# Router logits by token quarters, turned by VectorE, in a fused retention and mixture-of-experts kernel

## The chip, the cores and the metric

The kernel runs on one core of a Trainium2 chip. The metric is the device time of one execution in microseconds (us), lower is better; times are medians of several runs on the same chip. The engines are TensorE (PE, matmuls; PEld is its loading of weights), VectorE (DVE), ScalarE (ACT), GpSimd (POOL) and SyncE (SP, which here issues DMAs).

## The reference

Eight batches and eight heads of retention (attention with a decay in place of the softmax), then a mixture of experts over the 4608 tokens, in which each expert takes at most 576:

```python
ret = scores * Dmat                       # scores = q k^T / 8, Dmat = gamma_h ** (i - j) for i >= j
x = (ret @ v) in the order (batch, token, head * dim)      # 4608 x 512
logits = x @ w_gate                       # 4608 x 8
for idx in np.argsort(-logits.flatten()): # greedy, best pair of token and expert first
    tok, e = idx // E, idx % E
    if assigned[tok] >= 0 or counts[e] >= cap: continue
    assigned[tok] = e; counts[e] += 1
for e in range(E):
    mask = assigned == e
    out[mask] = np.maximum(x[mask] @ w1[e], 0.0) @ w2[e]
```

## The kernel before

**Attention** works on four batch pairs (bp) of two batches, each with four head pairs (hp) of two heads: 16 units u = 4 bp + hp, each in two half units, h = 2u + g, numbered 0 to 31. One half unit makes on TensorE the outputs from the running states (`from_states`), the scores of the next blocks (`scores`), two steps of the state (`update`) and the outputs from masked scores (`from_blocks`). VectorE multiplies the scores with the decay (`masks`, tile `am`, in even halves also `at`), ScalarE copies states (`st`) and outputs (`keep`, into the transposed outputs `xT`), GpSimd scales queries (`qin`) and keys (`ks`) two units ahead. The states of an odd half are multiplied into the same bank from which `at` has to be read first. The loads of a unit are issued by SyncE four units ahead, in one order with the writes of finished rows.

**What else is to be done in a half unit** stands in the table `fill`: `at(h, f, ...)` puts a call behind the work of half h (h - 0.5: ahead of its copy). For each finished batch pair bp these calls, from half g = 8 (bp + 1) on, turn the outputs into rows (`rows`, VectorE, two blocks of 128 tokens into one of four `raw` buffers), write these to the scratch array xd (`rows_out`, SyncE), and make the **logits** of its nine token blocks: `logits` multiplies three blocks at a time, each head pair into its own 32 partitions of a PSUM bank, and copies that with ScalarE into `lt`; `logits2` transposes it with TensorE, and VectorE sums the four head pairs into `Lg` [token in block, block, expert]. Then `best` (six VectorE steps: highest logit, its expert), `count_tables` (tables G of how many candidates each token reaches), `count_first_pe` (nine matmuls that count them), `first_digits` and `first_table` (digits of the logits and tables FT for the search). The last batch pair goes through the same steps behind the last half unit, with nothing beside them.

**Routing and experts.** `search_first` finds the threshold of the first expert by digits, `members` and `listing` number its tokens (a token's number is 128 times its block plus its partition), rows are gathered from xd, and `moe` does the eight expert layers, with the search for the next expert on VectorE beside the matmuls. Their order is written by a small planner with fixed costs.

Of the kernel before, what the change touches and what calls it, by code (L numbers as in the profile page):

```python
# [66 lines left out]
def route_consts():  # L67
    p = np.arange(128)

    def ordered(k, sh):  # L70
# [4 lines left out]
    rows = lambda a: np.broadcast_to(a.reshape(1, -1), (128, a.size))  # L75
    f = np.concatenate([p[:, None] < p[None, :], p[:, None] > p[None, :], rows(8 - np.arange(8)), rows(np.arange(32)),
                        rows(32*(4*(np.arange(20) % 5) + np.arange(20)//5)), rows(np.arange(36)),
                        rows(np.append(ordered(128, FIRST[0])[1:], np.finfo(np.float32).max)), rows(np.arange(1, 129)),
                        p[:, None]], axis=1)
# [6 lines left out]
class Route:  # L86
# [14 lines left out]
    def setup(s):  # L101
# [32 lines left out]
        s.pc = take(1)  # L134
        s.Gt = T("G0", [9, 128], BF16)
# [292 lines left out]
    def listing(s, p):  # L428
# [16 lines left out]
        for g0, g1 in ((0, 9),) if p else ((0, 5), (5, 9)):  # L445
# [3 lines left out]
            if p:  # L449
                V.tensor_scalar(rh[:, 1, :, c], rh[:, 2, :, c], s.pc, None, op0=ALU.mult)  # L450
            else:
                nc.scalar.activation(rh[:, 1, :, c], rh[:, 2, :, c], AF.Copy, scale=s.pc)
# [17 lines left out]
        for a in range(4):  # L470
            V.scalar_tensor_tensor(s.idx[32*a:32*a+32], lo[:, 0, 0, 5*a:5*a+5], 128.0, lo[:, 0, 1, 5*a:5*a+5], op0=ALU.mult, op1=ALU.add)
        if early:
            s.room(cn)
        if p >= PIECES:
            s.quarter = pool.tile([128, 20], I32, name="quarter", bufs=2)
            V.tensor_scalar(lo[:, 1], lo[:, 0], 4.0, None, op0=ALU.mult)
            for a in range(4):
                V.scalar_tensor_tensor(s.quarter[32*a:32*a+32], lo[:, 1, 0], 128.0, lo[:, 1, 1], op0=ALU.mult, op1=ALU.add)
                if a:
                    V.tensor_scalar(s.quarter[32*a:32*a+32], s.quarter[32*a:32*a+32], float(a), None, op0=ALU.add)  # L480
# [48 lines left out]
def attention(tc, nc, P, qk, vk, cst_d, wg_d, rf, xd, Lg, raw):  # L529
# [45 lines left out]
    R = Route(P['c'], P['a'], P['ps'], Lg, P['ident'])  # L575
# [96 lines left out]
    def logits(bp, b0, b1):  # L672
        lt = LT[bp, b0] = P['w'].tile([128, 640], F32, name="lt", bufs=1)
        for z0, z1 in ((b0, b1),) if b1 - b0 < 5 else ((b0, 6.5), (6.5, b1)):
            z0, z1 = int(128*z0), int(128*z1)
            pl = bank("pT", [128, z1 - z0])
            for i, (x, y, b) in enumerate(runs(z0, z1)):
                for hp in range(HP):
                    nc.tensor.matmul(pl[32*hp:32*hp+32, x-z0:y-z0], wg[:, hp, b, :], XT[bp][:, hp, x:y],  # L679
                                     start=(i == 0), stop=True, skip_group_check=True)  # L680
            nc.scalar.activation(lt[:, z0-128*b0:z1-128*b0], pl, AF.Copy)

    def logits2(bp, b0, b1):
        lt = LT[bp, b0]
        n, c0 = b1 - b0, bp*NB + b0
        pt = bank("pT", [128, n, 4, 32]) if n < 5 else here[0].rearrange("p x q -> p (x q)")[:, :128*n].rearrange("p (j h e) -> p j h e", h=4, e=32)
# [555 lines left out]
```

## Time and profile before

| | |
|---|---|
| median of 3 runs | 630.12 us (628.62 to 633.43) |
| profiled execution | 635.54 us, span 633.8 us, 14777 instructions |
| mean granted TensorE clock | 0.983 |
| TensorE busy | 603.6 us, 95% of the span |
| VectorE, ScalarE, GpSimd busy | 428.5, 257.2, 240.5 us |
| DMA in the first 160 us | 48.31 MB, 302 GB/s on the mean |

The profile is of one execution, which took longer than the three timed ones. Busy shares are means over stages with different limits: the first 145 us are attention, the rest is routing and experts. Full speed of TensorE's clock is 1.00; it has two levels, 1.2 and 2.4 GHz.

### The profile page before, as it was taken

Reading aid. Unit: us, or ns where it says so; the run is one execution under the profiler, and the core shown is the slowest. Engines: PE = TensorE matmul, PEld = TensorE weight load, DVE = VectorE, ACT = ScalarE, POOL = GpSimd, SP = SyncE. Lnnn points to the kernel's source line nnn. Section 1 sums busy time; section 2 is a strip of 40 time slices with the busy share of each in tenths; the row PEclk is TensorE's granted clock in tenths of the full one; section 3 lists DMA queues with packets and bytes.
Section 4 is the critical chain, followed back from the end, with each engine's and each line's share of the span. In section 5 each row is a group of like instructions: output and inputs, shape, how many; then the busy total and the mean of one; then the engine's idle time right before and its main releaser. Section 6 shows DMA issues by size and latency. Waiting matters only on the chain.

```text
span 633.8 us, 14777 instructions
## 1 busy us (share of the span) xinstructions
PE 603.6 (95%) x5724; PEld 518.4 (82%) x5724; DVE 428.5 (68%) x1506; ACT 257.2 (41%) x449; POOL 240.5 (38%) x295
## 2 busy tenths in 40 slices
PE   7899998998999999999999999999999895999995
PEld 5788887775698889879978987997898694989984
DVE  6746868888889888878867875885787641453400
ACT  2344432342553545535452562555162331343310
POOL 5787555405411541532431342143127566021011
PEclk9999998999999999999999999999999997899998
DMA  9999899845877698696993898499477423240011
GB/s 327 407 377 397 280 353 322 264 121 168 205 205 160 208 265 201 212 269 146 240 229 113 189 234 233 87 244 238 141 154 214 154 87 95 72 166 25 1 36 40
DMA packets 51225, 124.83 MB, mean 197 GB/s; under 512 B 7187, under 2 KB 22419, under 8 KB 51155
## 3 DMA queue, kind: packets, MB, share of 16 engines
q1 hardware_dynamic: 37906, 80.10, 36.7%
q0 software_dynamic: 13104, 43.53, 30.5%
q8 instruction: 45, 0.74, 0.5%
q10 hardware_dynamic: 144, 0.26, 0.1%
q14 instruction: 26, 0.20, 0.1%
HBM read 80.35 MB, written 18.87 MB: 157 GB/s over the span
## 4 chain that ended last, share of the span: by engine, by line
PE 54%; issue 17%; DMA 15%; POOL 8%; DVE 3%; SPq 1%; ACT 0%; POOLq 0%; DVEq 0%
PE ph L1061 23%; PE py L1102 21%; DMA vin<-in_vk 8%; POOL xg L981 6%; DMA xd<-raw 2%; POOL out_y L1079 2%; DMA kin<-in_qk 2%; DMA qin<-in_qk 2%; PE r L353 2%; PE pt L1025 2%; PE sc L603 1%; PE px L647 1%; DMA raw<-in_w 1%; PE pT L679 1%; PE pS L624 1%
## 5 line engine op out<-in xcount | busy, mean ns | idle before, releaser
L1102 PE MATMUL py<-w2h,hb 128*128 128x512 f32 x576 | 187.8, 398 | 1.1 <-issue 1.1
L1061 PE MATMUL ph<-xh,w1h 128*128 128x320 f32 (+1 forms) x512 | 153.2, 303 | 2.0 <-issue 1.7
L1061 PE MATMUL ph<-xl,w1h 128*128 128x320 f32 (+1 forms) x512 | 150.8, 299 | 3.1 <-issue 3.1
L1061 PE MATMUL ph<-xh,w1l 128*128 128x320 f32 (+1 forms) x512 | 150.4, 299 | 2.8 <-issue 2.7
L1102 PE MATMUL py<-w2l,hb 128*128 128x512 f32 (+1 forms) x320 | 125.1, 391 | 0.9 <-issue 0.9
L1102 PEld LDWEIGHTS py<-w2h,hb 128*128 128x128 f32 x576 | 104.4, 188 | 24.6 <-issue 3.2
L1061 PEld LDWEIGHTS ph<-xl,w1h 128*128 128x128 f32 x512 | 97.3, 192 | 5.3 <-issue 5.1
L1061 PEld LDWEIGHTS ph<-xh,w1h 128*128 128x128 f32 x512 | 97.3, 192 | 4.6 <-issue 3.3
L1065 ACT ACTIVATE hb<-ph 128x256 fp32r<-128x256 f32 (+1 forms) x128 | 51.6, 409 | 117.5 <-PE ph L1061 99.9
L1061 PEld LDWEIGHTS ph<-xh,w1l 128*128 128x128 f32 x512 | 97.2, 192 | 1.6 <-issue 1.6
L1079 POOL DMA_INDIRECT out_y<-yt,idx x40 | 40.5, 1011 | 148.2 <-ACT yt L1119 90.6
L1068 DVE SCALAR_TENSOR_TENSOR hb<-ph,hb 128x256 fp32r<-128x256 f32 (+1 forms) x192 | 57.7, 351 | 43.0 <-ACT hb L1065 39.5
L1102 PEld LDWEIGHTS py<-w2l,hb 128*128 128x128 f32 (+1 forms) x320 | 56.7, 177 | 13.4 <-issue 0.7
L588 POOL TENSOR_TENSOR qin<-qin,cst 128x512 f32<-128x512 f32 (+1 forms) x48 | 47.1, 1009 | 42.3 <-DMA qin<-in_qk 38.3
L1119 ACT ACTIVATE yt<-py 128x512 f32<-128x512 f32 x32 | 19.1, 598 | 99.1 <-PE py L1102 60.4
L612 DVE TENSOR_TENSOR am<-sc,cst 128x1024 f32<-128x1024 f32 x32 | 39.1, 1221 | 29.3 <-PE sc L603 29.1
L627 ACT ACTIVATE st<-pS,cst 128x128 f32<-128x128 f32 x64 | 23.5, 368 | 80.0 <-PE pS L624 80.0
L962 POOL DMA_DIRECT2D w2l<-raw x24 | 21.7, 905 | 71.9 <-ACT w2l L961 32.1
L993 POOL DMA_INDIRECT xg<-xd,idx x30 | 30.2, 1005 | 43.0 <-DVE room L494 16.1
L981 POOL DMA_INDIRECT xg<-xd,quarter x36 | 36.5, 1013 | 12.9 <-issue 10.7
L603 PE MATMUL sc<-qin,kin 64*128 64x128 f32 x512 | 38.1, 289 | 1.7 <-POOL qin L588 1.4
L962 POOL DMA_DIRECT2D w1l<-raw x23 | 21.2, 935 | 43.5 <-ACT w1l L961 35.1
(196 smaller groups left out, 943.4 us busy)
## 6 DMA issues: line engine op xcount, KB each, us to landing
raw<-in_w SPq DMA_DIRECT2D x56, 512.0 KB
w2l<-raw POOLq DMA_DIRECT2D x24, 512.0 KB
w1l<-raw POOLq DMA_DIRECT2D x23, 512.0 KB
qin<-in_qk SPq DMA_DIRECT2D x14, 576.0 KB
kin<-in_qk SPq DMA_DIRECT2D x14, 576.0 KB
vin<-in_vk SPq DMA_DIRECT2D x14, 576.0 KB
nin<-in_vk SPq DMA_DIRECT2D x14, 512.0 KB
xd<-raw SPq DMA_DIRECT2D x36, 128.0 KB
```

Of the source, the lines that this page charges most:

```text
L588: nc.gpsimd.tensor_tensor(x, x, e[:, None, :n].to_broadcast([128, (b-a)//n, n]), op=ALU.mult)
L603: nc.tensor.matmul(t[:, h, 128*j:128*j+128], blk(k, 4*g+j)[r], blk(q, 4*g+j)[r], start=(j == 0), stop=True, skip_group_check=True)
L612: nc.vector.tensor_tensor(a, SC[u, g].rearrange("p h (j q) -> p h j q", q=128), m1[:, u % HP, :, None, :].to_broadcast([128, 2, 4, 128]), ...
L627: nc.scalar.activation(s, p, AF.Copy, scale=ss[:, u % HP, c:c+1])
L962: add = lambda: nc.gpsimd.dma_start(lo, raw, accum_op=ALU.add)
L981: nc.gpsimd.indirect_dma_start(out=t[:, k, :], out_offset=None, in_=xq[:, :], in_offset=bass.IndirectOffsetOnAxis(ap=quarters[e][:, v:v+1] ...
L993: nc.gpsimd.indirect_dma_start(out=xg[:n, j, :], out_offset=None, in_=xd[:, :], in_offset=bass.IndirectOffsetOnAxis(ap=found[e][:n, j:j+1] ...
L1061: T.matmul(ps, w, x, start=(k == 0), stop=(k == 11))
L1065: A.activation(hb[:, f, c], ps, AF.Relu)
L1068: V.scalar_tensor_tensor(hb[:, f, to+a:to+b], ps[:, a:b], 0.0, hb[:, f, 256*s+a:256*s+b].bitcast(F32), op0=ALU.max, op1=ALU.subtract)
L1079: st = nc.gpsimd.indirect_dma_start(out=out[:, :], out_offset=bass.IndirectOffsetOnAxis(ap=found[e][:n, t:t+1], axis=0), in_=y[:n], in_off ...
L1102: T.matmul(ps[:m], a, w, start=(k == 0), stop=(k == last), skip_group_check=True)
```

## The change

The logits of a batch pair are made by token quarters. In a first step (z = 0) the pair's first 512 tokens go as four groups of 128 columns into four groups of 32 partitions, in a second (z = 1) the other 640 as four groups of 160; the four head pairs are added in PSUM. One turn of 32x32 squares by VectorE (`turned`) brings the result into `Lg`, whose rows are now 32 wide, with 8 in use. The copy by ScalarE, the transposes by TensorE and the sums are gone. Tokens lie in another order over partitions and columns, so the numbers for the lists change (`blocks()`, `p % 32`, 32 in place of 128). The tables G share the buffer of the later ones.

In the table `fill`, `best` comes into half g + 5 (it was at the front of g + 6), the tables G into g + 6, 6, 7, the digits into g + 7 (it was g + 8), the tables FT up to one half earlier. For the third pair all of that stands two halves earlier still, in one piece for nine blocks, and its turns into rows begin one half earlier. The logits of the last pair's first three head pairs are put into halves 27, 28 and 30; only those of the fourth remain behind its outputs.

```diff
-    def logits(bp, b0, b1):
-        lt = LT[bp, b0] = P['w'].tile([128, 640], F32, name="lt", bufs=1)
-        for z0, z1 in ((b0, b1),) if b1 - b0 < 5 else ((b0, 6.5), (6.5, b1)):
-            z0, z1 = int(128*z0), int(128*z1)
-            pl = bank("pT", [128, z1 - z0])
-            for i, (x, y, b) in enumerate(runs(z0, z1)):
-                for hp in range(HP):
-                    nc.tensor.matmul(pl[32*hp:32*hp+32, x-z0:y-z0], wg[:, hp, b, :], XT[bp][:, hp, x:y],
-                                     start=(i == 0), stop=True, skip_group_check=True)
-            nc.scalar.activation(lt[:, z0-128*b0:z1-128*b0], pl, AF.Copy)
-
-    def logits2(bp, b0, b1):
...
-        for j in range(n):
-            nc.tensor.transpose(pt[:, j], lt[:, j*128:(j+1)*128], ident)
-        nc.vector.tensor_reduce(Lg[:, c0:c0+n, :], pt[:, :, :, 0:8].rearrange("p j h e -> p j e h"), axis=AX.X, op=ALU.add)
+    def logits(bp, z, hps=range(HP)):
+
+        if z == 0 and 0 in hps:
+            LT[bp] = P['ps'].tile([128, 288], F32, name="lt", tag="t", bufs=1)
+        x, n, o = ((0, 128, 0), (512, 160, 128))[z]
+        for hp in hps:
+            for g in range(4):
+                nc.tensor.matmul(LT[bp][32*g:32*g+32, o:o+n], wg[:, hp, g // 2, :], XT[bp][:, hp, x+n*g:x+n*g+n],
+                                 start=(z == hp == 0), stop=True, skip_group_check=True)
+
+    def turned(bp, z0, z1):
+        a, b = (0, 4)[z0], (4, 9)[z1]
+        nc.vector.transpose(Lg[:, bp*NB+a:bp*NB+b].rearrange("p c e -> p (c e)"), LT[bp][:, 32*a:32*b])
...
-        n = 6 if end else 9
-        digits, best = R.first_digits(c, c+n), R.best(c, c+n)
+        digits, best = R.first_digits(c, c+9), R.best(c, c+9)
...
-        for h, x in ((1, (0, 1)), (2, (2, 3)), (3, (4, 5)), (4, (6, 7)), (5, (8,))):
+        for h, x in enumerate(((0, 1), (2, 3), (4, 5), (6, 7), (8,)), not end):
...
+        for z in range(2):
+            at(g+z, logits, bp, z)
+        at(g+2, turned, bp, 0, 1)
         for i in range(3):
-            at(g+2*i, logits, bp, 3*i, 3*i+3)
-            at(g+2*i+1, logits2, bp, 3*i, 3*i+3)
-            at(g + ((4, 5, 6) if end else (6, 7, 7))[i], R.count_tables, c+3*i, c+3*i+3)
+            at(g + ((4, 4, 5) if end else (6, 6, 7))[i], R.count_tables, c+3*i, c+3*i+3)
         for i in range(6):
-            fill[g + (4 if end else 6)].insert(i, (next, (best, None)))
-        if end:
-            last = R.best(c+6, c+9)
-            for i in range(6):
-                fill[g+6].insert(i, (next, (last, None)))
...
+            at(g + (3 if end else 5), next, best, None)
...
+    for hp in range(HP - 1):
+        for z in range(2):
+            at(27 + hp + (hp == 2), logits, NP-1, z, (hp,))
...
-    logits2(bp, 0, 4)
-    logits(bp, 4, 9)
+    logits(bp, 1, (HP-1,))
+    turned(bp, 0, 0)
     rest(R.count_first(27, 31))
+    turned(bp, 1, 1)
     R.first_table(3, 4, 6)
     here[0] = P['pp'].tile([128, 2, 512], F32, name="px", tag="px", bufs=2)
-    logits2(bp, 4, 9)
```

VectorE in halves 21 and 22, the second batch pair, before (`raw` is the turn of block 8, `Lg` the sum of logits, `am` and `at` the masks, m to oh the six steps of `best`, G a counting table):

```order
L700 STREAM_TRANSPOSE raw<-xT 128x4x4x32
L689 TENSOR_REDUCE Lg<-pT 128x24
L612 TENSOR_TENSOR am<-sc,cst 128x1024
L616 TENSOR_TENSOR at<-px,cst 128x256
L211 TENSOR_REDUCE m<-Lg 128x9
L213 TENSOR_TENSOR t_468<-Lg,m 128x72
L215 TENSOR_TENSOR t_468<-t_468,decb 128x72
L219 TENSOR_SCALAR m<-m 128x9
L221 TENSOR_REDUCE mx_469<-t_468 128x9
L223 TENSOR_TENSOR oh<-t_468,mx_469 128x72
L238 TENSOR_TENSOR G_493<-rc_f,m 128x384
L612 TENSOR_TENSOR am<-sc,cst 128x1024
```

The same place in the changed kernel:

```order
L700 STREAM_TRANSPOSE raw<-xT 128x4x4x32
L216 TENSOR_REDUCE m<-Lg 128x9
L218 TENSOR_TENSOR t_468<-Lg,m 128x72
L220 TENSOR_TENSOR t_468<-t_468,decb 128x72
L224 TENSOR_SCALAR m<-m 128x9
L226 TENSOR_REDUCE mx_469<-t_468 128x9
L228 TENSOR_TENSOR oh<-t_468,mx_469 128x72
L617 TENSOR_TENSOR am<-sc,cst 128x1024
L621 TENSOR_TENSOR at<-px,cst 128x256
L243 TENSOR_TENSOR G<-rc_f,m 128x384 x2
L617 TENSOR_TENSOR am<-sc,cst 128x1024
```

The six steps of `best` moved from behind the masks of half 22 to ahead of them; the sum of logits is gone.

TensorE in the last half unit and behind it, before (px from `am` and `at` are the last outputs, G the counts of the third pair, xT at the end the row transposes of the last pair):

```order
L679 MATMUL pT<-xT,wg 32x256 x8
L647 MATMUL px<-am,vin 64x128 x8
L653 MATMUL px<-at,vin 64x64 x4
...
L688 MATMUL pT<-ident,lt 128x128 x4
L679 MATMUL pT<-xT,wg 32x320 x8
L688 MATMUL px<-ident,lt 128x128 x5
L718 MATMUL pT<-ident,xT 128x128 x16
```

And in the changed kernel, from the logits of the third head pair in half 30 on:

```order
L684 MATMUL lt<-xT,wg 32x128 x4
L684 MATMUL lt<-xT,wg 32x160 x4
L643 MATMUL px<-qin,st 64x128 x8
L643 MATMUL px<-qin,st 64x64 x4
L684 MATMUL lt<-xT,wg 32x128 x4
L652 MATMUL px<-am,vin 64x128 x8
L658 MATMUL px<-at,vin 64x64 x4
L684 MATMUL lt<-xT,wg 32x160 x4
L718 MATMUL pT<-ident,xT 128x128 x16
```

Nine transposes and three of four parts of the last pair's logits left the place behind the last outputs; the counts of the third pair moved ahead of the last half.

## Rows read from the trace of the kernel before

**Rows 1.** Busy us and counts by stretch; then granted clock, DMA share, GB/s.

```profile
90.00:100.00 10.00, 7.24 (x147) 6.38 (x150) 4.84 (x9) 3.10 (x8) 6.24 (x6) 0.98 1.02 352
100.00:110.00 10.00, 9.94 (x189) 8.69 (x189) 9.76 (x18) 3.04 (x7) 5.22 (x7) 0.85 1.00 310
```

**Rows 2.** Timeline of PE, second pair: start us, us, instructions, [idle before].

```profile
81.15 0.86 PE L679 MATMUL pT<-xT,wg 128*32 128x128 f32 x16
81.94 0.78 PE L638 MATMUL px<-qin,st 64*64 64x128 f32 x24
...
85.47 0.55 PE L688 MATMUL pT<-ident,lt 128*128 128x128 f32 x3
85.94 0.45 PE L638 MATMUL px<-qin,st 64*64 64x128 f32 x8
...
89.13 0.86 PE L679 MATMUL pT<-xT,wg 128*32 128x64 f32 x16
...
109.32 0.78 PE L638 MATMUL px<-qin,st 64*64 64x128 f32 x24
...
114.23 0.45 PE L638 MATMUL px<-qin,st 64*64 64x128 f32 x8
```

**Rows 3.** Chain that ended last, up to the hole: start us, us, what.

```profile
80.66 8.66 DMA vin<-in_vk
...
89.34 8.10 DMA xd<-raw
```

**Rows 4.** Timeline of all engines around the hole.

```profile
93.92 0.45 PE L638 MATMUL px<-qin,st 64*64 64x128 f32 x8
...
97.56 0.71 DVE L700 STREAM_TRANSPOSE raw<-xT 128x512 f32<-128x512 f32 x1 [3.96 <-DMA xd<-raw]
98.19 0.22 DVE L689 TENSOR_REDUCE Lg<-pT 128x24 f32<-128x96 f32 x1
...
98.33 1.21 DVE L612 TENSOR_TENSOR am<-sc,cst 128x1024 f32<-128x1024 f32 x1
98.88 2.93 POOL L588 TENSOR_TENSOR qin<-qin,cst 128x512 f32<-128x512 f32 x3 [2.96 <-DMA qin<-in_qk]
...
99.80 0.20 DVE L211 TENSOR_REDUCE m<-Lg 128x9 f32<-128x72 f32 x1
...
99.93 1.34 PE L638 MATMUL px<-qin,st 64*64 64x128 f32 x24 [2.76 <-DVE at L616]
...
100.30 1.15 DVE L215 TENSOR_TENSOR t<-t,decb 128x72 bf16<-128x72 bf16 x1
...
101.77 2.04 POOL L593 TENSOR_TENSOR ks<-nin,cst 128x512 f32<-128x512 f32 x2
102.00 0.90 DVE L223 TENSOR_TENSOR oh<-t,mx 128x72 bf16<-128x72 bf16 x1
...
104.91 0.45 PE L638 MATMUL px<-qin,st 64*64 64x128 f32 x8
```

**Rows 5.** Timeline of DVE, first and last of the six steps, third pair.

```profile
125.27 0.19 DVE L211 TENSOR_REDUCE m<-Lg 128x6 f32<-128x48 f32 x1
...
126.19 0.21 DVE L223 TENSOR_TENSOR oh<-t,mx 128x48 bf16<-128x48 bf16 x1
```

**Rows 6.** Timeline from the last half unit to the search.

```profile
133.38 0.93 PE L638 MATMUL px<-qin,st 64*64 64x128 f32 x24
134.23 1.26 PE L679 MATMUL pT<-xT,wg 128*32 128x256 f32 x16
...
136.81 0.77 ACT L662 ACTIVATE xT<-px 128x320 f32<-128x320 f32 x2 [0.67 <-DVE FT L198]
...
139.74 1.04 PE L718 MATMUL pT<-ident,xT 128*128 128x128 f32 x8
...
142.01 0.37 PE L247 MATMUL px<-oh,G 128*128 128x8 bf16 x9
...
142.42 0.17 DVE L252 TENSOR_TENSOR f<-px,room 128x8 bf16<-128x8 f32 x1
```

More of the change, by code (lines that the diff above doesn't have):

```diff
@@ L75, in route_consts, with blocks @@
     rows = lambda a: np.broadcast_to(a.reshape(1, -1), (128, a.size))
+    def blocks():
+        c, g = np.arange(36)[None, :], p[:, None] // 32
+        z = c % 9
+        return 36*(c // 9) + np.where(z < 4, 4*g + z, 16 + 5*g + z - 4)
     f = np.concatenate([p[:, None] < p[None, :], p[:, None] > p[None, :], rows(8 - np.arange(8)), rows(np.arange(32)),
-                        rows(32*(4*(np.arange(20) % 5) + np.arange(20)//5)), rows(np.arange(36)),
+                        rows(32*(4*(np.arange(20) % 5) + np.arange(20)//5)), blocks(),
                         rows(np.append(ordered(128, FIRST[0])[1:], np.finfo(np.float32).max)), rows(np.arange(1, 129)),
-                        p[:, None]], axis=1)
+                        p[:, None], p[:, None] % 32], axis=1)
     return np.ascontiguousarray(f, dtype=np.float32)
@@ L133, in setup @@
         s.dec, i32, i20, cc, s.cand128, k128 = [take(n) for n in (8, 32, 20, 36, 128, 128)]
-        s.pc = take(1)
-        s.Gt = T("G0", [9, 128], BF16)
+        s.pc, s.pm = take(1), take(1)
+        s.Gt = s.G.rearrange("p (a b) k -> p a (b k)", a=9)
         V.tensor_copy(s.decb, s.dec)
@@ L449, in listing @@
             if p:
-                V.tensor_scalar(rh[:, 1, :, c], rh[:, 2, :, c], s.pc, None, op0=ALU.mult)
+                V.tensor_scalar(rh[:, 1, :, c], rh[:, 2, :, c], s.pm, None, op0=ALU.mult)
             else:
-                nc.scalar.activation(rh[:, 1, :, c], rh[:, 2, :, c], AF.Copy, scale=s.pc)
+                nc.scalar.activation(rh[:, 1, :, c], rh[:, 2, :, c], AF.Copy, scale=s.pm)
             V.tensor_tensor(rh[:, 0, :, c], rh[:, 2, :, c], s.cc[:, :, c], op=ALU.mult)
@@ L477, in listing @@
             for a in range(4):
-                V.scalar_tensor_tensor(s.quarter[32*a:32*a+32], lo[:, 1, 0], 128.0, lo[:, 1, 1], op0=ALU.mult, op1=ALU.add)
+                V.scalar_tensor_tensor(s.quarter[32*a:32*a+32], lo[:, 1, 0], 32.0, lo[:, 1, 1], op0=ALU.mult, op1=ALU.add)
                 if a:
@@ L574, in attention @@
     decays(0)
-    R = Route(P['c'], P['a'], P['ps'], Lg, P['ident'])
+    R = Route(P['c'], P['a'], P['ps'], Lg[:, :, 0:8], P['ident'])
     G = 16*NB
@@ L766, in attention @@
                 at(g+h+1, rows_out, bp, x[0], a)
+        for z in range(2):
+            at(g+z, logits, bp, z)
+        at(g+2, turned, bp, 0, 1)
         for i in range(3):
-            at(g+2*i, logits, bp, 3*i, 3*i+3)
-            at(g+2*i+1, logits2, bp, 3*i, 3*i+3)
-            at(g + ((4, 5, 6) if end else (6, 7, 7))[i], R.count_tables, c+3*i, c+3*i+3)
+            at(g + ((4, 4, 5) if end else (6, 6, 7))[i], R.count_tables, c+3*i, c+3*i+3)
         for i in range(6):
-            fill[g + (4 if end else 6)].insert(i, (next, (best, None)))
-        if end:
-            last = R.best(c+6, c+9)
-            for i in range(6):
-                fill[g+6].insert(i, (next, (last, None)))
-        at(g + (6.5 if end else 7.5), lambda c: later.append(R.count_first_pe([c, c+3, c+6], lambda: here[0][:, 0, 352:360])), c)
-        at(g + (6 if end else 8), rest, digits)
+            at(g + (3 if end else 5), next, best, None)
+        at(g + (5.5 if end else 7.5), lambda c: later.append(R.count_first_pe([c, c+3, c+6], lambda: here[0][:, 0, 352:360])), c)
+        at(g + (5 if end else 7), rest, digits)
         for i, t in enumerate(tables[:3] if bp else tables):
-            at(g + ((6, 6, 7) if end else (9, 10, 12, 13, 15))[i], t)
+            at(g + ((5, 5, 6) if end else (8, 9, 11, 13, 15))[i], t)
+    for hp in range(HP - 1):
+        for z in range(2):
+            at(27 + hp + (hp == 2), logits, NP-1, z, (hp,))
     def ahead(u):
@@ L823, in attention @@
             elif g:
-                logits(NP-1, 0, 4)
+                logits(NP-1, 0, (HP-1,))
             from_blocks(u, g)
@@ L1185, in build @@
         P['ident'] = P['ident_r'].bitcast(F32)
-        Lg = P['c'].tile([128, 36, 8], F32, name="Lg")
+        Lg = P['c'].tile([128, 36, 32], F32, name="Lg")
         mix = Mixer()
```

5 lines of the change are left out of this document (1 added, 4 removed).

## Prediction, made before the result was known

> **What bounds the kernel now.** I read the page first, then the busy time by stage, then the matmul engine's (TensorE's) own timeline, and last the chain that ended last. The expert layers, from about 165 us to the end, keep their instructions and their order; of them only a few of VectorE's routing steps read the logits at a wider spacing. So the question is the first 145 us, attention and the start of routing.
>
> In most of that stage TensorE is the bound: its stretches are full, except one. From 90 to 100 us it is busy 7.24 of 10 us, and in the next stretch its granted clock is 0.85 [rows 1]. The reader is to see two kinds of half unit. Without logits an even half lasts 3.19 us (85.94 to 89.13). The logits of three token blocks take 0.79 us there (81.15 to 81.94), and their three transposes 0.47 us in the odd half behind it (85.47 to 85.94) [rows 2].
>
> The hole at 97 us is not made by TensorE. The chain of work that ended last runs there through DMA alone: a load of 8.66 us, then a write of turned rows to the scratch array, 8.10 us, issued at 89.34 [rows 3]. VectorE's turn of block 8 of the second batch pair needs the buffer which that write empties, and waits 3.96 us, until 97.56. Behind it stand the masks of half 22, and TensorE waits 2.76 us for them, to 99.93. The half unit that follows then takes 4.98 us (99.93 to 104.91) [rows 4], where the one at 81.94 took 3.53 without its transposes [rows 2]: 1.45 us more, in the stretch whose clock is partly at the lower of 1.2 and 2.4 GHz [rows 1].
>
> **The change part by part.**
>
> *Logits of the first three pairs.* A pair loses three logits groups and three groups of transposes, 3 x (0.79 + 0.47) = 3.78 us on TensorE. It gains 32 matmuls, 16 over 128 columns and 16 over 160. Four of them, in four column groups, stand for one of the old rounds; 0.79 us for 384 columns is 2.06 ns a column, so 512 columns cost 1.05 us and 640 cost 1.32 us, 2.37 us a pair. More weight loads speak for a higher price: were each round as slow as the old whole group without any overlap between rounds, 3 us; the lower end is 2.0 us, from the rate at which the two long groups at the end pass. I take 2.37, since the row is of the same form: a pair saves 1.4 us (0.8 to 1.8). ScalarE loses its copies of the logits, which nobody waited for before the last pair.
>
> *VectorE's turn in place of its sums.* Three sums of 0.22 us become one turn of 288 columns. A turn of 512 takes 0.71 us [rows 4], so 0.40 by columns, between 0.22 and 0.71. It lies beside TensorE's work: nothing.
>
> *What the savings of the first two pairs are worth.* They come before 97.56, and the wait there ends when the write lands. Loads and writes stand in one order in SyncE's queue, which the change leaves alone, and the chain that leads to this landing has no TensorE in it [rows 3]. TensorE comes to the hole some 2.8 us sooner and waits that much longer: 0 us in the profiled execution. If the hole were not there, they would be worth 2.8 us.
>
> *Best experts ahead of the masks.* In halves 13 and 21 the six steps that find each token's best expert now stand between the turn of block 8 and the next masks; before they stood behind the masks. In half 21 this is just behind the wait, and TensorE is idle and waits for these masks. Alone, the six steps take 1.13 us (125.27 to 126.40) [rows 5]. In the second pair, beside GpSimd's scaling of the queries, they took 3.10 us (99.80 to 102.90): one of them 1.15 and one 0.90 us, where the shortest in the last pair take 0.2 [rows 4, 5]. GpSimd starts that scaling at 98.88, when its load lands, 0.61 us after the turn ends at 98.27, and goes on with the keys at 101.77 [rows 4]. So the price is +1.1 to +3.0 us; I take +2.0, since two steps can pass before GpSimd begins. The idle time before it gets longer too; I leave the cost of the lower clock at what it is now, 1.45 us, with up to 2 us more for the range.
>
> The Trainium skill, SBUF — State Buffer, section "SBUF: two separate sides", says that VectorE and GpSimd share one pair of ports, and that whichever starts first holds it for its whole instruction against a VectorE step that reads two operands from SBUF or runs in a two-port mode. The row of 1.15 us agrees: it ends where a GpSimd instruction could have ended. By that rule the steps of this kind, four of six, could each wait out one GpSimd instruction, which speaks against putting them ahead of the masks.
>
> *The later halves, 24 to 30.* Here the chain is TensorE's. By the prices above: half 24 +0.26 (1.05 for 0.79), half 25 +0.85 (1.32 for 0.47), half 26 -0.79, half 27 -0.47, half 28 -0.79, half 29 -0.47. The logits of the last pair's first three head pairs are new here, in halves 27, 28 and 30, 2.37 / 4 = 0.59 each. The nine counting matmuls of the third pair come into half 30 from half 31, 0.37 [rows 6]. Sum: -1.41 + 1.78 + 0.37 = +0.74. Half 25 took 4.91 us (109.32 to 114.23) [rows 2], with 3.53 + 0.47 to be expected: 0.91 lost, while VectorE did the digits of the second pair. These now come a half earlier; I count half of it back, -0.45 (0 to -0.91).
>
> *The end of attention.* From the start of the last half at 133.38 to the first comparison of the search at 142.42 it takes 9.04 us [rows 6]. After: states 0.85 (133.38 to 134.23), logits of one head pair 0.26, blocks 1.32 (to the copy's start at 136.81, less the old logits), two copies 0.77, logits 0.33, the turn of 160 columns 0.22, then 2.27 for the sixteen row transposes that still stand ahead of the count (139.74 to 142.01), count 0.41, and three handoffs of about 0.1: 6.73. That is -2.3 us (-1.5 to -3). The first of these transposes takes the bank of the logits, so it starts only behind the turn; VectorE's own steps in that time fit under the 2.27. From here on, search and expert layers only move.
>
> *The rest.* The numbers in the token lists change (32 where it was 128), not their count. VectorE's turns of the third pair come a half earlier, with buffers emptied by writes that are in flight then: 0, up to +2. Every step on the logits reads 8 of 32 columns: 0, for rows of eight stay whole.
>
> Sum against the profiled 635.54 us: 0 + 2.0 + 0.74 - 0.45 - 2.3 = 0.0, so 635.5. The median of the three runs lies 5.4 us under it; I carry the difference over, and forecast **630.1 us, no change**. A measurement here tells about 1% (6.3 us) from nothing.
>
> **The rivals.**
>
> *The hole is smaller in the timed runs.* The profiled execution is 5.4 us longer than the median, and the hole with its slow half unit makes up 2.76 + 1.45 = 4.2 of such a difference; that speaks for it. Against it: DMA is full in the stretch, 1.02 [rows 1], whoever measures. Then the first two pairs are worth 2.8 us and the end 2.0 (0.74 - 0.45 - 2.3), less up to 1.8 where the best experts still make masks late: -4.8 to -3.0, some **626.3**.
>
> *Slower: VectorE's steps are locked out in the hole.* The rows show the third and the sixth step held [rows 4]; if the second and the fourth are held as well, each for one GpSimd instruction of 0.98 us (2.93 / 3) [rows 4], the masks come 4 x 0.98 + 2 x 0.2 = 4.3 us late, not 2.0. TensorE has then idled 8 to 10 us in place of 2.76, and a whole further half unit of 3.2 us runs at half clock: +3.2. Together 2.3 + 3.2 = 5.5 over the forecast, **635.6**. It decides once GpSimd begins before the third of the six steps.
>
> *The logits do not get cheaper*, each round of four paying its weight loads in full: 3 us a pair in place of 2.37. With the hole this reaches only halves 24 to 30, by 0.6 x 2: **631.3**.
>
> **How the numbers follow.** Forecast 0.47, smaller hole 0.33, locked out 0.12, dearer logits 0.08. The range takes the forecast with its unknowns (+1.0 or -0.9 for the six steps, +-0.8 for the end), the smaller hole down to -4.8, and half of the way to the slower rival: 625.4 to 633.0. Faster by over 1% needs more than any sum here gives: 0.06. Slower by over 1% is the slower rival with a wait for a buffer in the third pair on top: 0.06. Within 1%: 0.88.
>
> **What would show it.** Matmuls of the logits at 1.05 and 1.32 us a pair. The wait of VectorE's turn still ending near 97 to 98 us, longer than 3.96, and masks starting 1 to 3 us behind it; the first comparison of the search some 6.7 us after the last half begins. The forecast is wrong if the write lands earlier because SyncE's queue runs ahead, if the clock stays low for more than one half unit, or if the expert layers change their length.

## The result, and the profile after

The changed kernel took **635.61 us** (median of 13 runs, 633.14 to 639.13), the kernel before 632.15 (13 runs, 628.62 to 634.80): ratio **1.0066** (95% interval 1.0040 to 1.0091). Forecast were 630.1 and a range of 625.4 to 633.0; the change costs 4.1 us (635.61 less 631.47, the median of 35 later runs of the kernel before), within the 1% that was called no change, but clear of zero. (The ratio stands for 4.2 us, the two medians themselves lie 3.5 apart; below, the 4.1 is used.) The profiled execution took 637.16 us (span 635.4, clock 0.982, 14841 instructions).

The stretches of the profile after; they answer to [rows 1]:

```profile
90.00:100.00 10.00, 7.69 (x160) 6.76 (x156) 5.05 (x9) 3.60 (x9) 6.18 (x7) 1.00 1.04 371
100.00:110.00 10.00, 6.81 (x108) 6.23 (x108) 8.18 (x16) 1.33 (x3) 6.51 (x6) 0.66 1.04 346
...
140.00:150.00 10.00, 7.23 (x80) 6.09 (x80) 7.09 (x30) 3.31 (x7) 2.02 (x3) 0.83 0.35 130
```

TensorE is now busy 6.81 us in the second stretch, where it was 9.94, and its granted clock there is 0.66, where it was 0.85. A third stretch with a low clock, 0.83, is new: the end of attention. The logits, on TensorE's timeline of the first and the second pair, answer to [rows 2]:

```profile
42.40 1.48 PE L684 MATMUL lt<-xT,wg 128*32 128x128 f32 x32
43.82 0.78 PE L643 MATMUL px<-qin,st 64*64 64x128 f32 x24
...
74.77 1.08 PE L684 MATMUL lt<-xT,wg 128*32 128x128 f32 x32
75.78 0.78 PE L643 MATMUL px<-qin,st 64*64 64x128 f32 x24
...
79.48 1.29 PE L684 MATMUL lt<-xT,wg 128*32 128x160 f32 x32
80.70 0.45 PE L643 MATMUL px<-qin,st 64*64 64x128 f32 x8
```

From start to start the second pair's two steps take 1.01 and 1.22 us (1.05 and 1.32 were forecast), the first pair's first step 1.42. The hole, on the timeline of all engines, answers to [rows 4]:

```profile
94.44 0.45 PE L643 MATMUL px<-qin,st 64*64 64x128 f32 x8
...
98.98 0.71 DVE L700 STREAM_TRANSPOSE raw<-xT 128x512 f32<-128x512 f32 x1 [4.01 <-DMA xd<-raw]
99.61 0.18 DVE L216 TENSOR_REDUCE m<-Lg 128x9 f32<-128x72 f32 x1
...
100.32 2.90 POOL L593 TENSOR_TENSOR qin<-qin,cst 128x512 f32<-128x512 f32 x3 [3.03 <-DMA qin<-in_qk]
100.59 1.08 DVE L228 TENSOR_TENSOR oh<-t,mx 128x72 bf16<-128x72 bf16 x1
101.59 1.21 DVE L617 TENSOR_TENSOR am<-sc,cst 128x1024 f32<-128x1024 f32 x1
...
103.19 1.35 PE L643 MATMUL px<-qin,st 64*64 64x128 f32 x24 [5.50 <-DVE at L621]
...
108.47 0.45 PE L643 MATMUL px<-qin,st 64*64 64x128 f32 x8
```

The turn of block 8 begins 1.42 us later than before (98.98 against 97.56), the masks stand 2.61 us behind it (0.77 before), and TensorE idles 5.50 us (2.76 before). The half unit that follows takes 5.28 us (103.19 to 108.47); the granted clock, read by single microseconds, is 0.50, the lower of the two levels, from 101 to 107 us and 1.00 again from 108 on. The end of attention, with the rows that answer to [rows 6]:

```profile
137.22 0.78 PE L643 MATMUL px<-qin,st 64*64 64x128 f32 x24
...
140.16 0.79 PE L684 MATMUL lt<-xT,wg 128*32 128x160 f32 x8 [0.54 <-ACT xT L667]
...
141.00 0.32 DVE L689 STREAM_TRANSPOSE Lg<-lt 128x128 f32<-128x128 f32 x1 [3.49 <-PE lt L684]
...
142.81 0.34 DVE L689 STREAM_TRANSPOSE Lg<-lt 128x160 f32<-128x160 f32 x1
...
143.30 1.06 PE L718 MATMUL pT<-ident,xT 128*128 128x128 f32 x8 [2.35 <-DVE Lg L689]
144.61 1.97 PE L718 MATMUL pT<-ident,xT 128*128 128x128 f32 x8 [0.25 <-ACT xT L722]
...
146.84 0.17 DVE L257 TENSOR_TENSOR f<-px,room 128x8 bf16<-128x8 f32 x1 [1.47 <-PE px L252]
```

From the last half unit to the first comparison it takes 9.62 us; 6.73 were forecast, 9.04 it took before. The reader is to see the first turn: its logits have been there since 138.4, but it waits 3.49 us, until 141.00, for the second step's matmuls. Both steps write one tile, and the turn is written behind the second. VectorE then needs 1.81 us until the second turn, and only behind that one do the row transposes get their bank, 2.35 us after TensorE had nothing else left. The second eight of them take 1.97 us where the first eight take 1.06: the granted clock, 1.00 until 144 us, is 0.50 from 145 to 148, after TensorE has idled. So the wait costs a second time: from the transposes' start to the first comparison it takes 3.54 us (143.30 to 146.84), where 2.68 were forecast (2.27 and 0.41).

### The profile page after: what moved, and what is told of

Its sections match the earlier page's. It is cut to its first block, busy times and chain, and to the rows that moved or that the text cites. A ratio compares the mean times of both kernels' runs of the same rounds, so it can differ in the third digit from the quotient of the medians.

```text
span 635.4 us, 14841 instructions
## 1 busy us (share of the span) xinstructions
PE 599.6 (94%) x5768; PEld 518.9 (82%) x5768; DVE 425.5 (67%) x1494; ACT 252.0 (40%) x437; POOL 241.5 (38%) x295
## 4 chain that ended last, share of the span: by engine, by line
PE 63%; issue 17%; DMA 9%; POOL 6%; DVE 3%; ACT 1%; SPq 1%; POOLq 0%; another core or an unknown queue 0%; DVEq 0%; ACTq 0%
PE ph L1061 24%; PE py L1102 21%; DMA vin<-in_vk 5%; PE sc L608 3%; POOL xg L981 3%; PE px L652 3%; POOL out_y L1079 2%; PE px L643 2%; PE pS L629 2%; PE pt L1025 2%; PE r L358 2%; PE lt L684 1%; DMA xd<-raw 1%; DMA qin<-in_qk 1%; DMA raw<-in_w 1%
```

## The experiments

Theory at first: the loss is the end and the place of the best experts, each some 2 us. Rivals: the write behind which VectorE waits, or the logits in two thick pieces. The last half unit is half 31, "the end" is the time from its start to the first comparison, and "lands" is when the turn of block 8 can start. Rows e are on one chip, where the kernel before has a median of 631.47 us (35 runs), the others on chips where it has 614.9 to 615.4 (17 to 29 runs); ratios are to that on the same chip. The last five columns are from one profiled execution each, which need not be a usual one of its kernel: m2's is the fastest of twelve, l2's the longest of six.

| kernel | ratio, 95% | lands | masks start behind it | TensorE idle ahead of half 23 | half 31 | end |
|---|---|---|---|---|---|---|
| before, first profile | | 97.56 | 0.77 | 2.76 | 133.38 | 9.04 |
| l3 before, second profile | | 94.69 | 0.78 | none | 128.66 | 9.05 |
| after, first profile | 1.0066 (1.0040 to 1.0091) | 98.98 | 2.61 | 5.50 | 137.22 | 9.62 |
| l4 after, second profile | 620.81 against 614.23 us, one run each | 95.73 | 2.62 | 2.99 | 134.79 | 9.94 |
| e1 best behind | 1.0063 (1.0035 to 1.0090) | 97.19 | 0.64 | 3.51 | 134.34 | 9.47 |
| e2 turn early | 1.0025 (0.9996 to 1.0053) | 96.12 | 2.62 | 3.87 | 134.35 | 6.43 |
| e3 block 8 later | 1.0037 (1.0006 to 1.0069) | no wait | | 0.45 | 130.60 | 9.86 |
| e4 all three | 1.0028 (0.9996 to 1.0059) | no wait | | none | 137.17 | 6.42 |
| l1 logits only | 1.0011 (0.9990 to 1.0032) | 97.32 | 0.63 | 2.37 | 133.22 | 7.27 |
| l2 best ahead only | 1.0055 (1.0038 to 1.0073) | 96.17 | 4.22 | 4.43 | 135.79 | 9.04 |
| m1 new end only | 1.0005 (0.9988 to 1.0023) | 95.04 | 0.78 | 0.17 | 132.20 | 7.72 |
| m2 best ahead of the turn | 0.9992 (0.9975 to 1.0010) | no wait | 0.63 | none | 130.54 | 6.43 |
| n1 best in three places | 1.0007 (0.9981 to 1.0032) | 95.13 | 0.64 | 0.65 | 131.59 | 6.43 |
| n2 weights earlier | 1.0022 (1.0000 to 1.0044) | 96.34 | 0.64 | 1.60 | 135.16 | 6.43 |
| n3 turn early, again | 1.0033 (1.0012 to 1.0053) | 94.91 | 2.64 | 2.42 | 132.46 | 6.43 |

**e2 and n3, the end.** The turn of the last pair's first columns, and what follows from it, are written ahead of the second logits step, and the first row transposes get the other bank:

```diff
-    tags[:] = ["sc", "t"]
-    logits(bp, 1, (HP-1,))
+    tags[:] = ["t", "sc"]
     turned(bp, 0, 0)
     rest(R.count_first(27, 31))
+    logits(bp, 1, (HP-1,))
     turned(bp, 1, 1)
```

> Only the end of attention is altered: the turn and the counting of the last pair's first four blocks are written ahead of the second logits step, so that they wait only for the first, and the row transposes begin in the bank that is free, not in that of the logits. Theory: the end lost its gain since the first turn waited until 141.00 for the second step's matmuls and the transposes 2.35 us for the second turn; the first comparison of the search then comes 6.7 to 7.2 us behind the start of the last half (9.62 as changed, 9.04 before), so 2.4 to 2.9 us off, ratio 1.002 to 1.003. Rival (the end is bound by the sixteen row transposes and VectorE's steps anyway): 9 us or more stay, ratio 1.006.

> The changed kernel with the early turn alone, once more. If the steps' place in the second pair cost 2 us: ratio 1.002 to 1.004, above the run with the steps ahead of the turn. If that difference was one between chips: 0.999 to 1.000.

Measured: 632.94 us for e2, 2.7 less than the changed kernel's 635.61; 616.91 for n3 on a chip where the kernel before takes 614.93: ratios of 1.0025 and 1.0033 where the change has 1.0066. The end was expected at 6.7 to 7.2 us. The timeline of e2:

```profile
134.35 0.78 PE L643 MATMUL px<-qin,st 64*64 64x128 f32 x24
...
135.55 0.32 DVE L689 STREAM_TRANSPOSE Lg<-lt 128x128 f32<-128x128 f32 x1 [0.92 <-PE lt L684]
...
138.01 1.18 PE L718 MATMUL pT<-ident,xT 128*128 128x128 f32 x8
138.12 0.35 DVE L689 STREAM_TRANSPOSE Lg<-lt 128x160 f32<-128x160 f32 x1 [0.68 <-PE lt L684]
...
140.78 0.17 DVE L257 TENSOR_TENSOR f<-px,room 128x8 bf16<-128x8 f32 x1
```

The turn waits 0.92 us in place of 3.49, the transposes no longer wait for VectorE, and the end takes 6.43 us, as in e4, m2, m4 and n1 to n3 (6.42 or 6.43 in each); l1, where VectorE's steps of the third pair stand ahead of the first turn, has 7.27. So the gain at the end that was forecast was to be had, by another order of these lines. With TensorE never out of work, the granted clock stays at 1.00, and the stretch from the first transposes to the first comparison takes 2.77 us (138.01 to 140.78). The intervals of e2 and of the change still overlap, so the 2.7 us are known only roughly; the end itself is the same in seven profiles.

**e1, e3, e4, the hole.** e1 puts the best experts of the first two pairs back behind the masks (at the front of g + 6); e3 turns block 8 of these pairs a half unit later, when its buffer is free; e4 is e1, e2 and e3 in one.

```diff
         for h, x in enumerate(((0, 1), (2, 3), (4, 5), (6, 7), (8,)), not end):
+            h += x[0] == 8 and not end
...
-            at(g + (3 if end else 5), next, best, None)
+            if end:
+                at(g + 3, next, best, None)
+            else:
+                fill[g + 6].insert(i, (next, (best, None)))
```

> One part undone: in the first two pairs the six steps of best stand behind the masks of the next half again (front of half g + 6), the rest as changed. Theory: the six steps cost the hole of half 22 some 2.0 us (99.61 to 101.59 in the changed kernel's trace), and TensorE's wait of 1.40 us before half 15 goes too, though it lies ahead of the hole and is swallowed there. So TensorE goes on about 1.7 us behind the end of the turn of block 8, as before, and the time falls by 2 us from 635.6, ratio to the kernel before 1.003 to 1.004. Rival (the write lands later because of the change, 98.98 in place of 97.56, and that is the loss): no more than 0.5 us back, ratio 1.006.

> The turn of block 8 of the first two pairs comes a half later, so that in half 21 nothing on VectorE ahead of the masks waits for a write; all else as changed, best still ahead of the masks. Theory: the hole swallowed what the logits of two pairs save, and made the clock fall; without it half 23 begins some 4 us sooner (98.7 to 100 in place of 103.19), at full clock, 5 to 6 us in all, of which a later wait for loads or buffers in the third pair may take 1 to 2 back: ratio 1.000 to 0.997. Rival (DMA bounds attention as a whole, so the hole only moves): a wait of like length in halves 22 to 29, ratio 1.005 or more.

> The three together: best behind the masks, block 8 a half later, the end altered. Theory: 5 to 6 us for the hole, 2.4 to 2.9 for the end, and the six steps no longer ahead of masks, about 0.5 more: 627 to 628, ratio 0.992 to 0.994, faster than the kernel before. Rival (DMA bounds attention): only the end's part is left, ratio 1.002 to 1.003.

e1 is no faster than the change (636.02 us, 1.0063, where 1.003 to 1.004 had been expected). In its profile the move does what it should at the hole: the masks start 0.64 us behind the turn, and the first comparison comes at 143.81, not 146.84. But the six steps (99.27 to 102.45, one of 1.16 and one of 0.90 us) and the tables behind them now stand ahead of the next masks, those of half 23, at 104.24, and TensorE waits 0.56 us for these. Why the median shows nothing isn't settled: from the first comparison on this execution is 2.9 us longer than the change's first (491.5 against 488.6), and a gain of 1 to 2 us lies inside the two intervals. The rival's ratio came true but its reason, a write that lands later, isn't seen: this one landed at 97.19, the change's at 98.98.

e3 has hardly a hole (0.45 us), and half 31 starts 6.6 us earlier in its profile, yet the median falls by only 0.9 us, where a ratio of 1.000 to 0.997 had been expected: its profiled execution, 631.99 us, is near the fastest of twelve that reach to 638.36. e4 has neither hole nor long end, and lies at 633.62 us, where 627 to 628 had been expected: in its profile VectorE's digits stand ahead of the masks of half 16, four of them at 0.96 to 1.23 us each (0.17 to 0.21 in the changed kernel's second profile), and half 16 takes 8.32 us (4.50 in the changed kernel's first profile). Half 24 goes the same way: 8.28 us, with a wait of 2.32 us for masks behind digits of 1.09 to 1.27 us. So of my theory of two separate losses of 2 us the end stands, by e2 and n3; for the hole no timed run of these shows it. In the profiles a VectorE step that is moved out of one mask's way stands in the way of a later one.

**l3 and l4, the two kernels once more.**

> The kernel before, one more look. If its first look was a slow one because of the hole ahead of half 23, this look has a span of 629 to 631 us with a wait of TensorE there of under 1.5 us and the first comparison of the search at 139.5 to 141 us. The rival: the hole is 2.5 to 3 us in every run, and what differs lies in the expert layers (the first comparison near 142.4 us again).

> The changed kernel, one more look. If the hole is the same in every run: TensorE idle for 5 to 6 us ahead of half 23 and the first comparison at 146 to 147 us. If it varies with the DMA queues: a hole between 2 and 6 us, and other halves that wait in its place; the end of attention takes 9.6 us in either case.

Timeline and stretch of the kernel before, second profile:

```profile
93.80 0.45 PE L638 MATMUL px<-qin,st 64*64 64x128 f32 x8
...
94.69 0.71 DVE L700 STREAM_TRANSPOSE raw<-xT 128x512 f32<-128x512 f32 x1 [1.08 <-DMA xd<-raw]
...
95.47 1.21 DVE L612 TENSOR_TENSOR am<-sc,cst 128x1024 f32<-128x1024 f32 x1
...
97.06 0.86 PE L638 MATMUL px<-qin,st 64*64 64x128 f32 x24
```

```profile
90.00:100.00 10.00, 9.99 (x207) 8.85 (x200) 8.10 (x15) 3.34 (x9) 7.32 (x9) 1.00 1.03 361
```

The hole of [rows 4] is not there: the write lands 2.87 us earlier, TensorE is busy 9.99 of 10 us, and half 31 starts at 128.66, not 133.38. So this hole isn't a fixed part of the kernel: it goes with the landing of the write. The first profile (635.54 us) is among the longest of the kernel before (628.43 to 637.94 in 35 runs), but the second was taken on another chip, and which of the two, the chip or the execution, moved the landing isn't shown. In the changed kernel's second profile the write lands at 95.73, also early, and TensorE still idles 2.99 us, since the six steps stand behind it. The first comparison of l3 comes at 137.71, ahead of the 139.5 to 141 expected; for l4 the second of its two cases came in.

**l1 and l2, each half of the change alone.** l1 takes the new logits and e2's end, with everything else in the halves of before; l2 is the kernel before with its best experts ahead of the masks (`at(g + 5, next, best, None)` in place of the front of g + 6, first two pairs).

> The changed kernel with the turn of the last pair's first columns written ahead of the second logits step (as in the run of that name, 632.9 us), and with the rows, best experts, counts, digits and tables of the first three pairs back in the halves where the kernel before has them: only the logits are new. Theory A, it is the moved steps of VectorE that cost the time in attention: the end gives its 2.6 us against the kernel before and nothing is lost ahead of it, 628 to 629.5 us, ratio about 0.996. Theory B, it is the logits packed into two halves, which leave the later halves without work that covers their masks: 632.5 to 633.5 us, as with the moved steps, ratio about 1.0025.

> The kernel before with one move of the change alone: the six steps for the best experts of the first two pairs a half earlier, ahead of the masks. Theory A (the moved steps cost): 633 to 635 us, ratio 1.003 to 1.006, and masks of half 22 that start 1 to 3 us behind the turn of block 8. Theory B (the logits cost): 631 to 632 us, ratio 1.000, since the six steps find room behind the transposes of the kernel before.

l2 alone costs 0.55%, 3.4 us (1.0055 x 615.23), nearly as much as the whole change; its masks start 4.22 us behind the turn, more than the 1 to 3 expected. Its timeline of VectorE, with TensorE's half 23:

```profile
96.17 0.71 DVE L700 STREAM_TRANSPOSE raw<-xT 128x512 f32<-128x512 f32 x1 [2.15 <-DMA xd<-raw]
...
97.58 1.22 DVE L215 TENSOR_TENSOR t<-t,decb 128x72 bf16<-128x72 bf16 x1
98.73 1.27 DVE L219 TENSOR_SCALAR m<-m 128x9 f32<-128x9 f32 x1
...
100.39 1.21 DVE L612 TENSOR_TENSOR am<-sc,cst 128x1024 f32<-128x1024 f32 x1
...
101.99 1.34 PE L638 MATMUL px<-qin,st 64*64 64x128 f32 x24 [4.43 <-DVE at L616]
```

GpSimd's scaling runs from 97.49 to 100.38 here; two of the six steps take 1.22 and 1.27 us beside it, in place of 0.2. That profiled execution (621.29 us) is the longest of its six, so its hole is more than the usual one. l1 lies between the theories: 0.1% over the kernel before although the end is 1.8 us shorter. So some 2.4 us (1.2 to 3.7 by its interval) go ahead of half 31, although the logits of the first pairs got cheaper. 1.9 of them have a place, if the price is as in l4: the last pair's logits in halves 27, 28 and 30 take 0.63, 0.63 and 0.62 us there.

**m2, the best experts ahead of the turn** (`fill[g + 5].insert(i, (next, (best, None)))` for the first two pairs, with e2's end), so that VectorE does them while it would wait for the write.

> The changed kernel with the early turn at the end (ratio 1.0025 with that alone), and with the six steps for the best experts of the first two pairs written ahead of the turn of block 8 in halves 13 and 21, so that VectorE does them while it would wait for the write. Theory A (what the moved steps cost is their place behind the wait and ahead of the masks): the hole loses 2 to 3 us, ratio 0.998 to 1.000. Theory B (the hole hangs on when the write lands, and the steps only fill it): ratio 1.0025 again, since the run with the steps back behind the masks gained nothing either.

```profile
93.12 0.22 DVE L216 TENSOR_REDUCE m<-Lg 128x9 f32<-128x72 f32 x1
...
94.14 0.23 DVE L228 TENSOR_TENSOR oh<-t,mx 128x72 bf16<-128x72 bf16 x1
...
94.75 0.71 DVE L700 STREAM_TRANSPOSE raw<-xT 128x512 f32<-128x512 f32 x1
95.38 1.19 DVE L617 TENSOR_TENSOR am<-sc,cst 128x1024 f32<-128x1024 f32 x1
...
96.95 0.78 PE L643 MATMUL px<-qin,st 64*64 64x128 f32 x24
```

The six steps take 1.17 us (93.12 to 94.29), none over 0.23, the masks follow the turn at once, and half 23 starts without a wait. 615.33 us, ratio 0.9992, where e2's schedule gave 1.0025 and, as n3, 1.0033: moving the six steps of two pairs ahead of their turns is worth about 0.4%, 2.5 us, with some 1 to 4 possible. That there is a gain is just shown (n3's interval begins at 1.0012, m2's ends at 1.0010), across two chips; n1, on n3's own chip, is 1.6 us faster than n3. In the first pair the new place gave nothing: there the turn waits for no write, the steps stand beside GpSimd's scaling and take 3.09 us (61.43 to 64.52), and TensorE waits 1.53 us ahead of half 15.

**n1 and n2, the rest of the places.** n1 is m2 with the first pair's steps behind the masks again and the third pair's ahead of its turn of block 8 (half 28); n2 besides loads the router's weights one head pair earlier (`if u == 1` in place of `u == 2`).

> The changed kernel with the early turn, the second pair's best experts ahead of the turn of block 8 (half 21), the first pair's back behind the masks (half 14), and the third pair's ahead of its turn of block 8 (half 28). If the place of these steps is the cause in every pair, the waits of TensorE ahead of halves 15 (1.5 us) and 29 (1.2 us) go: 1 to 2.5 us less than with the second pair's alone, ratio 0.995 to 0.998. If not, 0.999 again, with new waits in other halves.

> As the run beside it, with the router's weights loaded one head pair earlier. The wait of 0.7 to 0.8 us ahead of the first logits in half 8 goes. If the first pair's saving was lost there, 0.5 to 0.8 us less, ratio under that of the run beside it by 0.001; if the loads behind them in the queue come later by the same, nothing, or a longer wait in halves 9 to 12.

Nothing more came: the waits ahead of halves 15 and 29 went, as expected, but others took their place. In n1 one of 0.96 us stands ahead of half 17, behind digits of 1.18 and 1.32 us beside GpSimd's scaling. Half 29 took 4.53 us (3.53 in m2); TensorE stands among its outputs there, 0.61 us of it for nothing that the profile shows. Half 30 took 5.63 us (4.71 in m2), because the third pair's turn of block 8, which the change has moved a half unit forward, waits for a write as well and makes the masks late. TensorE's outputs, VectorE's turn and TensorE's scores in n1:

```profile
125.03 0.54 PE L652 MATMUL px<-am,vin 128*64 128x128 f32 x5 [0.61 <-issue]
125.04 0.71 DVE L700 STREAM_TRANSPOSE raw<-xT 128x512 f32<-128x512 f32 x1 [1.79 <-DMA xd<-raw]
...
127.84 1.16 PE L608 MATMUL sc<-qin,kin 64*128 64x128 f32 x16 [1.43 <-DVE am L617]
```

In n2 the first logits step takes 1.01 us (41.55 to 42.56) and half 22 starts at 92.91 (93.44 in n1); the write lands at 96.34, and TensorE waits 1.60 us: what was saved is swallowed in the hole, as the prediction had it. The third pair's turn of block 8 waits 2.83 us for its write in n2, TensorE behind it 2.07 us for masks, the granted clock is 0.50 from 130 to 133 us, and half 30 takes 7.85 us (127.31 to 135.16).

**m1, the new end on the kernel before**, all else untouched; the first three head pairs' logits in half 30 (`at(30, logits_last, z, range(HP - 1))`), two copies to the narrow logits.

> The kernel before, with one part of the change alone, at the end: the last pair's logits by token quarters (its first three head pairs in half 30, the fourth in the last half and behind it), turned by VectorE, the first turn written ahead of the second logits step, and each turned block copied to the narrow logits. The other three pairs keep their logits, sums and schedule. If the end is additive, it gives the 2.6 us that the run with the early turn showed, less 0.4 us for two copies and 0.5 for the matmuls in half 30: ratio 0.996 to 0.998, and 6.5 to 7 us from the start of the last half to the first comparison. If the saving at the end needs the rest of the change: ratio 1.000.

A miss: 1.0005. The end falls by 1.3 us only (7.72; the row transposes wait 0.89 us for the turn's bank), and half 30 takes 5.44 us in place of 3.19, since the 24 matmuls in one piece take 1.61 us there (130.59 to 132.20), not the 0.5 that I had put down, and a wait for masks of 0.57 comes ahead. It says nothing against the end; it says that the last pair's logits have to be paid somewhere.

**m3 and m4, every second write on ScalarE's queue** (`(nc.scalar if a % 2 else nc.sync).dma_start`), m3 on the kernel before, m4 on m2.

> The kernel before, with every second write of turned rows issued on ScalarE's queue in place of SyncE's. Theory: the hole ahead of half 23 is the delay in SyncE's one queue, where writes stand ahead of loads. Then the turn of block 8 waits for under 0.5 us, no hole is left in the profile, and the time is at or under the fastest runs of the kernel before: ratio 0.994 to 0.998. Rival: the DMA engines' rate sets the landing, not the queue, or ScalarE's issuing makes the states late: ratio 1.000 to 1.01.

> The changed kernel with the early turn at the end, the best experts ahead of the turn of block 8, and every second write on ScalarE's queue. If what the change lost in attention is the hole alone, it is now faster than the kernel before by the end and the cheaper logits: 2.6 + 1 to 3 us, ratio 0.990 to 0.995. If it stays at 1.000 or more, the loss is not in the hole but in halves that TensorE now passes with less work to cover VectorE's masks.

Ratios 1.0069 (1.0046 to 1.0092) and 1.0077 (1.0054 to 1.0100). VectorE no longer waits for a write in either, but TensorE comes to half 22 five to nine us later there (98.81 and 103.05), so that the one queue makes the landing late isn't shown. ScalarE stands still while it issues. Its timeline in m3, and TensorE's:

```profile
90.47 2.64 ACTq L708 DMA_DIRECT2D xd<-raw  x2
93.21 0.37 ACT L627 ACTIVATE st<-pS,cst 128x128 f32<-128x128 f32 x1 [2.97 <-DVE FT L198]
...
93.63 0.45 PE L624 MATMUL pS<-vin,ks 128*64 128x64 f32 x8 [1.04 <-ACT st L627]
```

Two issues take 2.64 us, the state's copy behind them is late, and TensorE waits 1.04 us for it. The rival that was on record for m3, a ScalarE held up by its issues, came true, in the time too; m4 therefore says nothing on where the changed kernel loses.

## Why the prediction was wrong, step by step

*The end of attention, -2.3 us: the step that failed.* It measured +0.58 (9.62 against 9.04), in the second profiles +0.89 (9.94 against 9.05): a miss of 2.9 to 3.2 us, most of the 4.1. The terms were about right, as e2 and its successors show (6.43 against 6.73 forecast). What I had put wrong is the order: I let the turn of 160 columns follow its logits by a handoff and had "VectorE's own steps in that time fit under the 2.27". In the program the first turn waits for the second step, so that VectorE's 1.81 us stand ahead of the second turn, and the bank and the transposes wait behind both. Some 0.8 us of the miss is the clock that falls in this wait: 3.54 us from the transposes to the first comparison, where e2 takes 2.77.

*The best experts, +2.0 us.* Right in place and, in the trace, in size: masks 2.61 us behind the turn in place of 0.77, +1.84. Timed, the place of these steps is worth 2.5 us (n3 against m2) to 3.4 (l2). By the Trainium skill, SBUF — State Buffer, section "SBUF: two separate sides", a step that reads two operands from SBUF, or runs in a two-port mode, waits out the GpSimd instruction that has the shared ports. The traces agree: held steps took 0.85 to 1.32 us beside GpSimd's scaling, the two-operand steps 0.20 to 0.23 without it, and the reductions, which read one operand, 0.18 to 0.23 beside it too. What I hadn't seen is that this goes for any place beside the scaling: in m2's first pair ahead of the turn, and in e1, as before the change, behind the masks (the six take 3.18 us there).

*The hole, 0 us for the savings of the first two pairs.* The result is right, the reason only half. TensorE was to come to the hole 2.8 us sooner; it came 0.52 later (94.44 against 93.92), in the second profiles 0.11 sooner. From half 8 to half 22 it takes 55.22 us against 55.05, in the second profiles 55.63 against 55.58. In half 8 it waits for the router's weights (0.80 us in l4), and in half 14 for masks behind the first pair's best experts (1.40 us ahead of half 15); without these two it takes 54.54 (n2, which still waits 0.79 us there for GpSimd's scaling), some 1 us less than the second profile of before, not 2.8. A misread row is in the 2.8 too: an odd half without transposes takes 3.67 us in the trace of before (66.02 to 69.69), and with its three transposes some 4.00, so these are worth 0.33, not the 0.47 of their row, and the two pairs' savings some 2.5.

*Halves 24 to 30, +0.29 in all (0.74 less 0.45).* In the first profiles 28.75 us against 28.47, +0.28, as forecast. In the second profiles it is +1.86 (29.85 against 27.99), and parts of that have a place: before's half 25 takes 4.00 us there, so that nothing of the 0.91 was left to win back, the changed kernel's half 24 waits 0.73 us for masks, and in half 28 TensorE stands 0.47 us for nothing that the profile shows. The third pair's turns, "0, up to +2", cost nothing in either profile of the changed kernel; in m2, n1 and n2, which come to them sooner, they wait 1.74, 1.79 and 2.83 us for a write.

*The rivals.* "The hole is smaller in the timed runs" was right that the hole can be absent (l3) and wrong on the price, since it counted the end's gain and savings that TensorE never had in hand. The measured time is the one that the slower rival named, 635.6, but by luck, not for its reason: of the four steps that it has held only the sixth was (1.08 us), the masks came 1.84 us later than before, not 4.3, and one half unit ran at the lower clock (5.28 us against 4.98 before), not two. Its price of 0.98 us for a GpSimd instruction was misread as well: the group of three shown in [rows 4] is two of 1.26 and 1.29 us and one of 0.47. "Dearer logits" is out: 2.23 us a pair.

*The anchor.* 630.1 was the median of three runs; 35 later ones give 631.5. Of the 5.5 us between forecast and result, 1.4 lie there, 2.9 in the end, and the rest, 1.2, in the hole and in what stands behind it. The first profiles bear that out: half 31 starts 3.84 us later than before, where the sum has 2.29 (2.0 + 0.74 - 0.45).

*What stays open.* With e2's end, 2.6 us shorter than before's, and the six steps out of the way, the changed kernel should be faster than before by about that; m2 and n1 lie at 0.9992 and 1.0007. Their half 31 starts at 130.54 and 131.59, against 128.66 in the second profile of before. Single executions can mislead here (l3's is 1.0 us under the median of its chip, m2's 2.1 under its own), but m2, n1 and l1 agree by their medians: what the end gains is lost ahead of half 31. Seen of this are the logits in halves 28 and 30, the wait in half 28 and 29, and thinner halves that give VectorE no time (even halves of 3.2 us); which share each has the runs don't settle, and no version that I ran is faster than the kernel before by more than its interval.

## What to carry to other kernels

Where two matmul groups write one tile, a reader of the first group that is written behind the second waits for both (3.49 us here, 0.92 with the read written first): follow such a read in the order of the program before a stage is summed by its operations. Side work on VectorE is free where VectorE itself waits and GpSimd isn't scaling: the same six steps cost 2.5 to 3.4 us behind a waiting instruction, and in m2's second pair nothing ahead of it; in its first pair, where the turn waits for nothing and GpSimd scales, they made TensorE wait 1.53 us. A wait for a DMA can differ from one execution to the next (TensorE's was 2.99 us in l4, 2.42 in n3, on one chip with the same order up to the last half): read a second profile before a term is built on it, and take the anchor from more than three runs.

## What the runs showed of the hardware that I had not expected

The kernel before took 631.5 us in the earlier runs and 615.2 us in the later ones, on other chips, and the expert layers make nearly all of it: from the first comparison to the end of the span 491.4 us in the first profile of before, 474.7 in the second (488.6 to 491.5 in the six earlier profiles, 474.3 to 475.0 in the eleven later ones). So on the later chips a difference between two kernels lies ahead of the first comparison. In the earlier runs TensorE waits late in the expert layers for nothing that the profile shows. Its waits from 490 us on in the first profile of before, then the same stretch in its first and its second profile:

```profile
PE ph L1061 <- issue: 7.5, 9, 1.8
PE py L1102 <- issue: 2.0, 4, 0.8
```

```profile
530.00:550.00 20.00, 14.23 (x74) 13.04 (x74) 6.36 (x17) 5.47 (x12) 5.76 (x7) 0.66 0.24 75
```

```profile
530.00:550.00 20.00, 20.00 (x90) 16.48 (x89) 10.51 (x18) 6.88 (x12) 3.26 (x6) 1.00 0.44 145
```

9.5 us of such waits, and a granted clock of 0.66 behind them, stand in the first profile, none in the second; all six earlier profiles have them (7.5 to 9.9 us), none of the eleven later ones. What is late there is not settled.
